# First batch's attention: transposes ahead of the fourth pair's scores, normalisation on GpSimd, copies shared with VectorE, one product matmul ahead of the last outputs

## The chip, the cores and the metric

The kernel runs on one core of a Trainium2 chip. Time is the device time of one launch in microseconds (us), the median of three runs. The engines are called as in the profile: PE is TensorE, DVE is VectorE, ACT is ScalarE, POOL is GpSimd, SP issues the DMAs. Each engine works through its own instructions in order and waits on semaphores for what the others produce.

## The reference

Two stages. The first is attention over 8 batches and 8 heads, sequence 576, head dimension 64, with a window of 32 keys: heads 0 to 3 look at the last 32 positions, heads 4 to 7 at every fourth of the last 128. The second is a dense feed-forward layer over all 4608 tokens, with an ELU between two products (512 to 2048 to 512), in float32.

```python
scores = scale * np.matmul(q, k.transpose(0, 1, 3, 2))
mask_plain = (rel >= 0) & (rel < window)
mask_dil = (rel >= 0) & (rel < window * dilation) & (rel % dilation == 0)
scores = np.where(masks[None, :, :, :], scores, -1000000000.0)
attn = np.exp(scores - np.max(scores, axis=-1, keepdims=True))
attn = attn / (np.sum(attn, axis=-1, keepdims=True) + 1e-09)
x = np.matmul(attn, v)                      # then to 4608 x 512
h = x @ w_in
g = np.where(h > 0.0, h, np.exp(np.minimum(h, 0.0)) - 1.0)
out = g @ w_out
```

## The kernel before, in words

**Feed-forward.** The tokens are worked in 9 chunks of 512 (`for c in range(NCH)`, L377), each in 16 blocks of the hidden dimension (L382). A block is a first product into the PSUM tile `h_ps` (`gemm1`, L271), ELU on ACT and DVE (`elu`, L282), and a second product into the four tiles `o_ps` (`gemm2`, L298), two blocks later. Chunk 0 multiplies float32 weights directly; from chunk 1 on, weights and activations are split into a high and a low part, and three products are added. The activations are split by `split_x` (L257): ACT casts to `xh` (L267), DVE takes the difference `xl` (L268). For chunk 1 it is called when the loop comes to that chunk, but its pieces of early columns are free to go as soon as their input is there.

**Weights.** They arrive as 64-bit floats and are put together as float32: the magnitude on ACT (`magnitude`, L98), then four DVE operations on bits (`convert`, L106 to L111). They are handled in pairs of two 128x512 blocks. In the order below pair 0 is converted in two halves (B0 for the first block of hidden units, C0 for the second) and pair 1 whole (D1); the others follow inside the loop.

**Attention of the first batch.** Eight heads are worked as four pairs. `first_attention` (L181) is a generator with five steps for a pair, and L348 gives the order in which the steps are issued, since everything in it is kept in program order on each engine: S (scores with the mask on PE, into PSUM tile `a` or `b`), M (row maximum and subtraction on DVE, L198 and L201; exp on ACT, L203), P (row sums, reciprocal and multiplication on DVE, L205, L169 to L171), T (12 transposing matmuls against the identity, L214, into `c` or `a`; then copies from PSUM into one of two tiles `pt`, eight per pair, on ACT, L223, or DVE, L221), O (12 output matmuls into `d` or `b`, L157; two copies into `x32` on ACT, L161 or L164). A is the magnitude of a weight pair on ACT, B, C and D its conversion on DVE. M of pairs 1 to 3 also starts the load of the weights (`load_w(hp, mx)`, L200), behind a small POOL copy (L84).

**Later batches.** Attention of batch c+1 is issued between the blocks of chunk c (L397). It has an order of its own, made by a scheduler, and its multiplication is on DVE for batch 1 and on POOL from batch 2 on (L243).

The identity is made on POOL at L339. PSUM tiles of the first batch come from the pool `ps_f`, which is closed before `ps_h`, `ps_o` and `ps_a` are opened (L357 to L360).

Of the kernel before, what the change touches and what calls it, by code (L numbers as in the profile page):

```python
# [10 lines left out]
F32 = mybir.dt.float32  # L11
# [5 lines left out]
ALU = mybir.AluOpType  # L17
# [6 lines left out]
P = 128  # L24
G = 32
QB = 3 * G
NU = S // QB
NPAIR = H // 2
NA = 3
GU = QB // G  # L30
TC = 512
# [13 lines left out]
def body(ctx: ExitStack, tc: tile.TileContext, q, k, v, masks, w_in, w_out, out):  # L45
# [5 lines left out]
    fp = ctx.enter_context(tc.tile_pool(name="fp", bufs=3))  # L51
    ps_first = ExitStack()
    ps_f = ps_first.enter_context(tc.tile_pool(name="ps_f", bufs=1, space=bass.MemoryType.PSUM))


    masks_sb = const.tile([QB, 2 * NU * 2 * G + QB], BF16, name="masks_sb")
# [20 lines left out]
    def mm(*args, **kw):  # L77
        inorder(nc.tensor.matmul(*args, **kw))  # L78
# [102 lines left out]
    def first_attention(hp, loaded):  # L181

        dil = hp >= NPAIR // 2
        qt, kt, vt = loaded
        if hp >= 2:
            sm = early[2 * (hp - 2) + 1][:QB, 2 * NU * D:2 * NU * (D + 2 * G)].rearrange("p (u j) -> p u j", u=2 * NU)
        else:
            sm = ap.tile([QB, 2 * NU, 2 * G], F32, name="sm")
        mx = ap.tile([QB, 2 * NU], F32, name="nmx", bufs=4)
        sums = ap.tile([QB, 2 * NU], F32, name="sums", bufs=4)  # L190
        s_ps = ps_f.tile([P, 2, TC], F32, name="ab"[hp % 2])[:QB, :, :NU * 2 * G]
        for h in range(2):
            mm(s_ps[:, h, :], ones_sb, mask_sb[:, int(dil), :], start=True, stop=False)
        scores([s_ps[:, h, :] for h in range(2)], qt, kt, False)
        yield
        s4 = s_ps.rearrange("p h (n j) -> p h n j", n=NU)
        mx4 = mx.rearrange("p (h n) -> p h n", h=2)
        inorder(nc.vector.tensor_reduce(out=mx4, in_=s4, op=ALU.max, axis=mybir.AxisListType.X))  # L198
        if hp > 0:
            load_w(hp, mx)  # L200
        inorder(nc.vector.tensor_tensor(out=sm.rearrange("p (h n) j -> p h n j", h=2), in0=s4,  # L201
                                        in1=mx4.unsqueeze(3).broadcast_to([QB, 2, NU, 2 * G]), op=ALU.subtract))
        inorder(nc.scalar.activation(out=sm, in_=sm, func=AF.Exp, scale=0.125))  # L203
        yield
        inorder(nc.vector.tensor_reduce(out=sums, in_=sm, op=ALU.add, axis=mybir.AxisListType.X))  # L205
        last_step[hp] = normalise(nc.vector, sm, sums, inorder).ins
        yield
        tr = transposed()

        t_ps = ps_f.tile([P, 2, TC], F32, name="ca"[hp % 2])  # L210
        for n in range(NU):
            for h in range(2):
                o = n % NA * QB
                mm(t_ps[h * 2 * G:(h + 1) * 2 * G, n // NA, o:o + QB], sm[:, h * NU + n, :], ident, start=True, stop=True)  # L214
        t4 = t_ps[:, :, :NA * QB].rearrange("p i (n q) -> p i n q", n=NA)
        for h in range(2):
            to = tr[:, h * NU:(h + 1) * NU, :].rearrange("p (i n) q -> p i n q", i=2)
            for c, r, m in ((0, 0, 2), (1, 0, 1), (1, 1, 1), (2, 0, 2)):
                cs, ks, rs = slice(c * G, (c + 1) * G), slice((c + r) * G, (c + r + m) * G), slice((h * 2 + r) * G, (h * 2 + r + m) * G)
                if hp == NPAIR - 1 and h == 1:  # L220
                    inorder(nc.vector.tensor_copy(out=to[ks, :, :, cs], in_=t4[rs, :, :, cs]))  # L221
                else:
                    inorder(nc.scalar.copy(out=to[ks, :, :, cs], in_=t4[rs, :, :, cs]))  # L223
        yield
        a_ps = ps_f.tile([P, 2, TC], F32, name="db"[hp % 2])
        yield outputs(0, hp, [(a_ps[:, i, :], i * NA, (i + 1) * NA) for i in range(NU // NA)], vt, tr, inorder)
# [41 lines left out]
                nc.vector.tensor_tensor(out=xl[hp][:, u], in0=src, in1=xh[hp][:, u].bitcast(F32), op=ALU.subtract)  # L268
                t0 += n

    def gemm1(c, f):  # L271
        h_ps = ps_h.tile([P, TC], F32, name="h_ps")
        i = 2 * f
        if c == 0:
            terms = [(full[i], x32[0][:, n, :TC], n) for n in range(NC)]
        else:
            terms = [(wh[i], x[n], n) for n in range(NC) for x in (xh, xl)] + [(wl[i], xh[n], n) for n in range(NC)]
        for t, (w, x, n) in enumerate(terms):
            mm(h_ps, w[:, n * P:(n + 1) * P], x, start=t == 0, stop=t == len(terms) - 1)
        return h_ps  # L280

    def elu(h_ps, first):  # L282
# [52 lines left out]
    for what in "m0 qk0 qk1 qk2 qk3 v0 v1 w0 v2 v3".split():  # L335
        i = int(what[-1])
        if what[0] == "m":
            nc.sync.dma_start(out=masks_sb, in_=masks)
            nc.gpsimd.tensor_copy(out=ident, in_=ones_sb)  # L339
        if what[0] == "w":  # L340
            load_w(i)
        for t, src in zip("qkv", (q, k, v)):
            if t in what:
                nc.sync.dma_start(out=rooms[i]["qkv".index(t)], in_=src[i])
    x32[0] = xp.tile([P, NPAIR, S], F32, name="x32", bufs=2)
    its = [first_attention(hp, rooms[hp]) for hp in range(NPAIR)]

    for what in "S0 S1 M0 M1 A0 S2 S3 P0 M2 T0 P1 M3 T1 O0 P2 T2 O1 P3 B0 T3 O2 O3 A1 C0 D1".split():  # L348
        i = int(what[1])
        if what[0] == "A":  # L350
            inorder(magnitude(i))
        elif what[0] in "BCD":
            last_conversion = convert(i, inorder, {"B": slice(0, DM), "C": slice(DM, 2 * DM), "D": slice(0, 2 * DM)}[what[0]])
        else:
            last_copy = next(its[i])
    ready = 2
    ps_first.close()  # L357
    ps_h = ctx.enter_context(tc.tile_pool(name="ps_h", bufs=2, space=bass.MemoryType.PSUM))
    ps_o = ctx.enter_context(tc.tile_pool(name="ps_o", bufs=TC // P, space=bass.MemoryType.PSUM))
    ps_a = ctx.enter_context(tc.tile_pool(name="ps_a", bufs=1, space=bass.MemoryType.PSUM))  # L360
    loaded[1, 0] = load_pair(1, 0)
# [13 lines left out]
                store(c, o_of.pop(c))  # L375

    for c in range(NCH):  # L377
        if c > 0:
            split_x(c)
        att = batch_attention(c + 1) if c + 1 < B else iter(())  # L380
        emitted = 0
        for f in range(NF):  # L382
            while c == 0 and ready < min(NF, f + AHEAD):
                with tc.issue_after(below[-1] if below else last_copy.ins):
                    magnitude(ready)
                with tc.issue_after(last_conversion.ins):
                    last_conversion = convert(ready)
                if ready + NR < NF:
                    load_w(ready + NR)
                ready += 1  # L390
            while c == 1 and split < min(NF, f + 2):

                with tc.issue_after(hidden[-4 if split < 2 else -1]):
                    split_w(split)
                split += 1
            pend.append((c, f, elu(gemm1(c, f), c == 0)))
            while emitted < (f + 1) * STEPS // (NF - 1):  # L397
                emitted += 1
                if c == 0 and emitted <= 2:
                    with tc.issue_after(last_step[NPAIR - 1]):  # L400
                        next(att, None)
                else:
                    next(att, None)
            flush(LAG)
# [60 lines left out]
```

## Time and profile before

| | |
|---|---|
| median of 3 runs | 923.32 us (921.7 to 923.71) |
| profiled execution | 923.31 us, span 921.5 us |
| PE busy | 902.1 us, 98% of the span |
| DVE, ACT, POOL busy | 525.9, 391.9, 42.2 us |
| first product matmul of chunk 0 starts | 34.08 us |

The span is the time from the first to the last recorded instruction; 1.8 us of the profiled execution lie around it. Times in the trace count from the span's start. PE is close to full, so the reading goes to the stretch before the first product, in which it is not. A matmul in float32 leaves two records in the trace: 12 matmuls are 24 records, a product of four matmuls is 8.

### The profile page before, as it was taken

The numbers are of one execution on the slowest core, as the hardware profiler recorded it, in microseconds if no ns is written. First come the engines' busy times: TensorE is split into PE (matmuls) and PEld (weight loads), VectorE is DVE, ScalarE is ACT, GpSimd is POOL, SyncE is SP. The second block draws the span as 40 slices with busy tenths as digits, with TensorE's granted clock in tenths as the row PEclk, the third lists the DMA queues.
The fourth block names the chain that finished last, engine by engine and source line by source line (L and its number), as shares of the span: only waits on it lengthen the run. The fifth ranks groups of instructions, "written<-read, shape, count | busy, mean of one in ns | idle before, by whom it ended". The sixth has DMA issues, their size and how long they took to land.

```text
span 921.5 us, 15903 instructions
## 1 busy us (share of the span) xinstructions
PE 902.1 (98%) x6504; PEld 688.3 (75%) x6504; DVE 525.9 (57%) x912; ACT 391.9 (43%) x1185; POOL 42.2 (5%) x34
## 2 busy tenths in 40 slices
PE   6799999999999999999999999999999999999998
PEld 4444445788878887888878887888788888888886
DVE  6699885965565545655475546655655443343332
ACT  4756762543344345344444335443443432233222
POOL 1000000010000000000010001000000000000000
PEclk8899999999999999999999999999999999999999
DMA  9964010211121112111211102111300010001001
GB/s 349 380 232 136 17 44 18 100 44 45 35 100 44 38 42 73 44 45 46 78 55 45 43 21 98 44 45 35 100 18 18 1 47 0 1 1 46 1 0 46
DMA packets 23800, 59.38 MB, mean 64 GB/s; under 512 B 2640, under 2 KB 2736, under 8 KB 23728
## 3 DMA queue, kind: packets, MB, share of 16 engines
q1 hardware_dynamic: 23728, 58.37, 18.7%
q8 instruction: 51, 0.84, 0.4%
q14 instruction: 21, 0.17, 0.1%
HBM read 48.92 MB, written 9.44 MB: 63 GB/s over the span
## 4 chain that ended last, share of the span: by engine, by line
PE 90%; ACT 5%; DVE 3%; DMA 1%; issue 1%; SPq 0%; ACTq 0%; DVEq 0%
PE h_ps L78 42%; PE o_ps L78 41%; PE a_ps L78 6%; ACT sm L242 3%; ACT pt L223 1%; DMA kt<-k 1%; PE b L78 1%; DVE sm L238 1%; DVE nmx L239 1%; ACT e L284 0%; DVE e L291 0%; ACT r L119 0%; ACT o L309 0%; DVE e L290 0%; PE c L78 0%
## 5 line engine op out<-in xcount | busy, mean ns | idle before, releaser
L78 PE MATMUL o_ps<-a,gh 128*128 128x512 f32 x640 | 258.4, 432 | 0.0
L78 PE MATMUL o_ps<-r,gh 128*128 128x512 f32 x512 | 205.8, 402 | 0.4
L78 PE MATMUL h_ps<-xh,r 128*128 128x512 f32 x512 | 200.5, 392 | 0.0
L78 PE MATMUL o_ps<-r,gl 128*128 128x512 f32 x512 | 199.7, 390 | 0.0
L78 PE MATMUL h_ps<-xl,r 128*128 128x512 f32 x512 | 199.3, 389 | 0.0
L284 ACT ACTIVATE e<-h_ps 128x512 f32<-128x512 f32 x144 | 85.5, 594 | 241.9 <-PE h_ps L78 241.7
L294 ACT CAST gh<-e 128x512 fp32r<-128x512 f32 x128 | 79.5, 621 | 191.2 <-DVE e L291 191.2
L290 DVE TENSOR_SCALAR e<-e 128x512 f32<-128x512 f32 x128 | 61.5, 481 | 164.1 <-ACT e L284 163.3
L78 PEld LDWEIGHTS o_ps<-a,gh 128*128 128x128 f32 x640 | 119.8, 188 | 45.8 <-issue 26.3
L295 DVE TENSOR_TENSOR gl<-e,gh 128x512 fp32r<-128x512 f32 x128 | 88.5, 692 | 75.0 <-PE o_ps L78 58.0
L242 ACT ACTIVATE sm<-sm,nmx 96x64 f32<-96x64 f32 x336 | 112.0, 335 | 32.0 <-DVE nmx L240 31.5
L78 PE MATMUL h_ps<-xh,a 128*128 128x512 f32 x448 | 119.7, 389 | 0.0
L78 PEld LDWEIGHTS o_ps<-r,gh 128*128 128x128 f32 x512 | 96.0, 187 | 26.2 <-ACT o L309 2.5
L78 PEld LDWEIGHTS o_ps<-r,gl 128*128 128x128 f32 x512 | 96.1, 188 | 21.1
L78 PEld LDWEIGHTS h_ps<-xh,r 128*128 128x128 f32 x512 | 96.1, 188 | 20.8 <-issue 0.2
L78 PEld LDWEIGHTS h_ps<-xl,r 128*128 128x128 f32 x512 | 96.1, 188 | 20.7 <-issue 0.7
L248 DVE STREAM_TRANSPOSE pt<-sm 32x384 f32<-32x384 f32 x168 | 95.5, 568 | 12.8 <-POOL sm L171 10.8
L78 PEld LDWEIGHTS h_ps<-xh,a 128*128 128x128 f32 x448 | 84.1, 188 | 17.5
L291 DVE SCALAR_TENSOR_TENSOR e<-h_ps,e 128x512 f32<-128x512 f32 x128 | 88.4, 691 | 3.9
L171 POOL TENSOR_TENSOR sm<-sm,sums 96x768 f32<-96x768 f32 x24 | 39.1, 1630 | 662.3 <-ACT e L284 321.6
L242 ACT ACTIVATION_READ_ACCUMULATOR sm<-sm,nmx 96x1 f32 x336 | 62.9, 187 | 0.0
L78 PE MATMUL h_ps<-x,a 128*128 128x512 f32 x128 | 60.3, 617 | 1.8 <-DVE gh L288 1.1
(82 smaller groups left out, 539.3 us busy)
## 6 DMA issues: line engine op xcount, KB each, us to landing
vt<-v SPq DMA_DIRECT2D x30, 384.0 KB, 3.2
kt<-k SPq DMA_DIRECT2D x30, 304.0 KB, 4.1
qt<-q SPq DMA_DIRECT2D x30, 288.0 KB, 3.6
r<-w_in SPq DMA_DIRECT2D x16, 512.0 KB, 7.0
r<-w_out SPq DMA_DIRECT2D x16, 512.0 KB, 7.1
out<-o SPq DMA_DIRECT2D x32, 256.0 KB, 2.9
out<-xl SPq DMA_DIRECT2D x4, 256.0 KB, 2.1
r<-v SPq DMA_DIRECT2D x2, 384.0 KB, 9.0
```

The lines of the kernel that those rows point to most:

```text
L78: inorder(nc.tensor.matmul(*args, **kw))
L171: return keep(eng.tensor_tensor(out=sm, in0=sm, in1=sums.unsqueeze(2).broadcast_to([QB, 2 * NU, 2 * G]), op=ALU.mult))
L223: inorder(nc.scalar.copy(out=to[ks, :, :, cs], in_=t4[rs, :, :, cs]))
L238: nc.vector.tensor_tensor(out=sm[:, h * NU:(h + 1) * NU, :].rearrange("p n j -> p (n j)"), in0=s_ps[h], in1=mask_sb[:, int(dil), :], op=AL ...
L239: nc.vector.tensor_reduce(out=nmx, in_=sm, op=ALU.max, axis=mybir.AxisListType.X)
L242: nc.scalar.activation(out=sm[:, u, :], in_=sm[:, u, :], func=AF.Exp, bias=nmx[:, u:u + 1], scale=0.125, accum_out=sums[:, u:u + 1])
L248: nc.vector.transpose(out=tr[ks, :, cs], in_=sm[cs, :, rs])
L284: nc.scalar.activation(out=e, in_=h_ps, func=AF.Exp)
L290: nc.vector.tensor_scalar(out=e, in0=e, scalar1=1.0, scalar2=-1.0, op0=ALU.min, op1=ALU.add)
L291: nc.vector.scalar_tensor_tensor(out=e, in0=h_ps, scalar=0.0, in1=e, op0=ALU.max, op1=ALU.add)
L294: nc.scalar.copy(out=gh, in_=e)
L295: nc.vector.tensor_tensor(out=gl, in0=e, in1=gh.bitcast(F32), op=ALU.subtract)
```

## The change

1. The order of the first batch's steps is another one. T0 stands before S3; P2 before M3; A0 behind M3 instead of behind M1; B0 behind T3 instead of before it.
2. The multiplication of pairs 0 to 2 goes to POOL; pair 3 keeps DVE.
3. The identity is made by a multiplication on POOL instead of a copy.
4. Of the copies behind the transposes, DVE takes over two of pair 1 (`c == 2`) and four of pair 2 (`h == 1`); it already had four of pair 3.
5. The transposes of pairs 0 and 2 get a PSUM pool of their own, `ps_c`. It is closed after B0, and `ps_h` is opened in its place, so that the first product's tile is there early.
6. The first product is a generator (`product1`), and one matmul of it (G0) is issued before the output step of pair 3 (O3).
7. `split_x(1)` is held behind the fourth last hidden block of chunk 0.

```diff
--- before.py
+++ after.py
@@ -51,6 +51,8 @@
     fp = ctx.enter_context(tc.tile_pool(name="fp", bufs=3))
     ps_first = ExitStack()
     ps_f = ps_first.enter_context(tc.tile_pool(name="ps_f", bufs=1, space=bass.MemoryType.PSUM))
+    ps_second = ExitStack()
+    ps_c = ps_second.enter_context(tc.tile_pool(name="ps_c", bufs=1, space=bass.MemoryType.PSUM, side="right"))
 
 
     masks_sb = const.tile([QB, 2 * NU * 2 * G + QB], BF16, name="masks_sb")
@@ -203,11 +205,13 @@
         inorder(nc.scalar.activation(out=sm, in_=sm, func=AF.Exp, scale=0.125))
         yield
         inorder(nc.vector.tensor_reduce(out=sums, in_=sm, op=ALU.add, axis=mybir.AxisListType.X))
-        last_step[hp] = normalise(nc.vector, sm, sums, inorder).ins
+        last = normalise(nc.vector if hp == NPAIR - 1 else nc.gpsimd, sm, sums, inorder)
+        if hp == NPAIR - 1:
+            last_step[hp] = last.ins
         yield
         tr = transposed()
 
-        t_ps = ps_f.tile([P, 2, TC], F32, name="ca"[hp % 2])
+        t_ps = (ps_c, ps_f)[hp % 2].tile([P, 2, TC], F32, name="ca"[hp % 2])
         for n in range(NU):
             for h in range(2):
                 o = n % NA * QB
@@ -217,7 +221,7 @@
             to = tr[:, h * NU:(h + 1) * NU, :].rearrange("p (i n) q -> p i n q", i=2)
             for c, r, m in ((0, 0, 2), (1, 0, 1), (1, 1, 1), (2, 0, 2)):
                 cs, ks, rs = slice(c * G, (c + 1) * G), slice((c + r) * G, (c + r + m) * G), slice((h * 2 + r) * G, (h * 2 + r + m) * G)
-                if hp == NPAIR - 1 and h == 1:
+                if hp >= 2 and h == 1 or hp == 1 and c == 2:
                     inorder(nc.vector.tensor_copy(out=to[ks, :, :, cs], in_=t4[rs, :, :, cs]))
                 else:
                     inorder(nc.scalar.copy(out=to[ks, :, :, cs], in_=t4[rs, :, :, cs]))
@@ -268,7 +272,8 @@
                 nc.vector.tensor_tensor(out=xl[hp][:, u], in0=src, in1=xh[hp][:, u].bitcast(F32), op=ALU.subtract)
                 t0 += n
 
-    def gemm1(c, f):
+    def product1(c, f):
+
         h_ps = ps_h.tile([P, TC], F32, name="h_ps")
         i = 2 * f
         if c == 0:
@@ -277,6 +282,11 @@
             terms = [(wh[i], x[n], n) for n in range(NC) for x in (xh, xl)] + [(wl[i], xh[n], n) for n in range(NC)]
         for t, (w, x, n) in enumerate(terms):
             mm(h_ps, w[:, n * P:(n + 1) * P], x, start=t == 0, stop=t == len(terms) - 1)
+            yield h_ps
+
+    def gemm1(c, f):
+        for h_ps in first if (c, f) == (0, 0) else product1(c, f):
+            pass
         return h_ps
 
     def elu(h_ps, first):
@@ -336,7 +346,7 @@
         i = int(what[-1])
         if what[0] == "m":
             nc.sync.dma_start(out=masks_sb, in_=masks)
-            nc.gpsimd.tensor_copy(out=ident, in_=ones_sb)
+            nc.gpsimd.tensor_tensor(out=ident, in0=ones_sb, in1=ones_sb, op=ALU.mult)
         if what[0] == "w":
             load_w(i)
         for t, src in zip("qkv", (q, k, v)):
@@ -345,17 +355,23 @@
     x32[0] = xp.tile([P, NPAIR, S], F32, name="x32", bufs=2)
     its = [first_attention(hp, rooms[hp]) for hp in range(NPAIR)]
 
-    for what in "S0 S1 M0 M1 A0 S2 S3 P0 M2 T0 P1 M3 T1 O0 P2 T2 O1 P3 B0 T3 O2 O3 A1 C0 D1".split():
+
+    for what in "S0 S1 M0 M1 S2 P0 M2 T0 S3 P1 P2 M3 A0 T1 O0 P3 T2 O1 T3 O2 B0 G0 O3 A1 C0 D1".split():
         i = int(what[1])
+        if what == "G0":
+            ps_second.close()
+            ps_h = ctx.enter_context(tc.tile_pool(name="ps_h", bufs=2, space=bass.MemoryType.PSUM, side="right"))
+            first = product1(0, 0)
         if what[0] == "A":
             inorder(magnitude(i))
         elif what[0] in "BCD":
             last_conversion = convert(i, inorder, {"B": slice(0, DM), "C": slice(DM, 2 * DM), "D": slice(0, 2 * DM)}[what[0]])
+        elif what[0] == "G":
+            next(first)
         else:
             last_copy = next(its[i])
     ready = 2
     ps_first.close()
-    ps_h = ctx.enter_context(tc.tile_pool(name="ps_h", bufs=2, space=bass.MemoryType.PSUM))
     ps_o = ctx.enter_context(tc.tile_pool(name="ps_o", bufs=TC // P, space=bass.MemoryType.PSUM))
     ps_a = ctx.enter_context(tc.tile_pool(name="ps_a", bufs=1, space=bass.MemoryType.PSUM))
     loaded[1, 0] = load_pair(1, 0)
@@ -375,7 +391,10 @@
                 store(c, o_of.pop(c))
 
     for c in range(NCH):
-        if c > 0:
+        if c == 1:
+            with tc.issue_after(hidden[-4]), tc.issue_after(below[-4]):
+                split_x(c)
+        elif c > 1:
             split_x(c)
         att = batch_attention(c + 1) if c + 1 < B else iter(())
         emitted = 0
```

The instruction orders show where this lands. The first place is the PE around the first transposes; `c<-ident,sm` are the transposes of pair 0, `b<-r_79` (before) and `b<-r_82` (now) the scores of pair 3. Before:

```order
L78 MATMUL a<-r_77 32x64 x36
L78 LDWEIGHTS masks_sb
L78 MATMUL b<-masks_sb 96x384
L78 LDWEIGHTS masks_sb
L78 MATMUL b<-masks_sb 96x384
L78 MATMUL b<-r_79 32x64 x36
L78 MATMUL c<-ident,sm 64x96 x12
```

Now:

```order
L80 MATMUL a<-r_80 32x64 x36
L80 MATMUL c<-ident,sm 64x96 x12
L80 LDWEIGHTS masks_sb
L80 MATMUL b<-masks_sb 96x384
L80 LDWEIGHTS masks_sb
L80 MATMUL b<-masks_sb 96x384
L80 MATMUL b<-r_82 32x64 x36
L80 MATMUL a<-ident,sm 64x96 x12
```

The transposes of pair 0 moved ahead of the mask matmuls and scores of pair 3, which now stand behind them.

The second place is DVE around the normalisation of pair 3, whose sums are read from `r_80` (before) and `r_83` (now). Copies into `pt` are those behind transposes, a `TENSOR_SCALAR` of 128x512 is the beginning of a half conversion of weight pair 0. Before:

```order
L171 TENSOR_TENSOR r_78<-r_78,sums 96x768
L205 TENSOR_REDUCE sums<-r_80 96x12
L169 TENSOR_SCALAR sums<-sums 96x12
L170 RECIPROCAL sums<-sums 96x12
L171 TENSOR_TENSOR r_80<-r_80,sums 96x768
L106 TENSOR_SCALAR a_201<-a_201 128x512
L108 TENSOR_SCALAR a_201<-a_201 128x512
L109 SCALAR_TENSOR_TENSOR a_201<-r_101,a_201 128x512
L268 TENSOR_TENSOR xl_1183<-x_106,xh_1182 128x64
L111 SCALAR_TENSOR_TENSOR a_201<-r_101,a_201 128x512
L268 TENSOR_TENSOR xl_1189<-x_106,xh_1188 128x64
L221 COPY pt_75<-a 64x6x32
```

Now:

```order
L225 COPY pt_78<-a 64x6x32 x2
L207 TENSOR_REDUCE sums<-r_83 96x12
L171 TENSOR_SCALAR sums<-sums 96x12
L172 RECIPROCAL sums<-sums 96x12
L173 TENSOR_TENSOR r_83<-r_83,sums 96x768
L225 COPY pt_79<-c 64x6x32
L225 COPY pt_79<-c 32x6x32 x2
L225 COPY pt_79<-c 64x6x32
L225 COPY pt_78<-a 64x6x32
L225 COPY pt_78<-a 32x6x32 x2
L225 COPY pt_78<-a 64x6x32
L108 TENSOR_SCALAR a_333<-a_333 128x512
```

Two copies of pair 1 (`pt_78<-a`, first row) stand ahead of pair 3's sums, four of pair 2 and four of pair 3 behind its multiplication, and the conversion begins behind all of them. The differences `xl` are gone from here.

The third place is the PE around the first product; `a<-ident` are the transposes of pair 3, `d` and `b` the outputs of pairs 2 and 3, `h_ps` the product. Before:

```order
L78 MATMUL b<-pt_75,vt 64x96 x12
L78 MATMUL a<-ident,r_80 64x96 x12
L78 MATMUL d<-pt_76,r_78 64x96 x12
L78 MATMUL b<-pt_75,r_80 64x96 x12
L78 MATMUL h_ps<-x_106,a_201 128x512 x8
L78 MATMUL a_ps_558<-kt,qt 32x64
```

Now:

```order
L80 MATMUL a<-ident,r_83 64x96 x12
L80 MATMUL d<-pt_79,r_81 64x96 x12
L80 MATMUL h_ps<-x_109,a_333 128x512
L80 MATMUL b<-pt_78,r_83 64x96 x12
L80 MATMUL h_ps<-x_109,a_333 128x512 x7
L80 MATMUL a_ps_562<-kt,qt 32x64
```

One of the eight matmuls of the first two products moved ahead of the twelve output matmuls of pair 3.

## Rows read from the trace of the kernel before

**Rows 1.** the page, busy time of each engine.

```profile
PE 902.1 (98%) x6504; PEld 688.3 (75%) x6504; DVE 525.9 (57%) x912; ACT 391.9 (43%) x1185; POOL 42.2 (5%) x34
```

**Rows 2.** four windows; columns: stretch, us, busy us of each engine, granted clock, DMA share, GB/s.

```profile
29.20:32.50 3.30, 1.14 (x21) 0.93 (x22) 2.19 (x7) 1.86 (x6) 0.00 (x0) 1.00 1.03 408
34.08:39.30 5.22, 5.22 (x6) 2.19 (x7) 4.15 (x7) 3.18 (x4) 0.00 (x0) 0.50 1.01 401
44.00:99.00 55.00, 55.00 (x354) 25.55 (x337) 53.12 (x76) 33.51 (x97) 0.00 (x0) 1.00 0.47 159
99.00:150.00 51.00, 49.95 (x250) 23.16 (x249) 36.09 (x52) 31.22 (x70) 0.00 (x0) 1.00 0.12 36
```

**Rows 3.** chain of waits, in order of time; columns: start us, us, what.

```profile
18.39 0.31 ACT pt L223
...
25.22 0.24 ACT xh L267
...
34.08 9.71 PE h_ps L78 x16
```

**Rows 4.** timeline of PE; columns: start us, us, work [idle before and releaser].

```profile
13.85 0.87 PE L78 MATMUL b<-masks_sb 96*96 96x384 bf16 x2 [3.62 <-DVE sm L171]
...
16.11 2.19 PE L78 MATMUL c<-ident,sm 96*64 96x96 f32 x24
...
25.49 1.23 PE L78 MATMUL a<-ident,r 96*64 96x96 f32 x23
```

**Rows 5.** timeline of DVE in the attention of the first batch.

```profile
12.26 0.95 DVE L171 TENSOR_TENSOR sm<-sm,sums 96x768 f32<-96x768 f32 x1
...
18.28 0.95 DVE L201 TENSOR_TENSOR r<-b,nmx 96x768 f32<-96x768 f32 x1
...
21.89 0.95 DVE L205 TENSOR_REDUCE sums<-r 96x12 f32<-96x768 f32 x1 [0.34 <-ACT r L203]
...
24.21 0.42 DVE L106 TENSOR_SCALAR a<-a 128x512 f32<-128x512 f32 x1
...
25.86 0.69 DVE L111 SCALAR_TENSOR_TENSOR a<-r,a 128x512 uint32<-128x512 uint32 x1
...
30.23 1.48 DVE L221 COPY pt<-a 64x192 f32<-64x192 f32 x4 [1.00 <-ACT pt L223]
...
35.09 0.69 DVE L106 TENSOR_SCALAR a<-a 128x1024 f32<-128x1024 f32 x1 [1.00 <-ACT a L98]
...
41.69 0.69 DVE L288 SCALAR_TENSOR_TENSOR gh<-h_ps,e 128x512 f32<-128x512 f32 x1 [1.99 <-ACT e L286]
```

**Rows 6.** timeline of ACT in the same stretch.

```profile
16.27 1.15 ACT L98 ACTIVATE a<-r 128x1024 f32<-128x1024 f32 x1 [4.49 <-DMA r<-w_in]
...
21.88 2.59 ACT L223 COPY pt<-a 64x192 f32<-64x192 f32 x8
...
33.92 3.21 ACT L98 ACTIVATE a<-r 128x1024 f32<-128x1024 f32 x3
```

**Rows 7.** POOL's first multiplication from its timeline, then all of them on the page.

```profile
172.53 1.93 POOL L171 TENSOR_TENSOR sm<-sm,sums 96x768 f32<-96x768 f32 x1 [154.03 <-ACT gh L294]
...
L171 POOL TENSOR_TENSOR sm<-sm,sums 96x768 f32<-96x768 f32 x24 | 39.1, 1630 | 662.3 <-ACT e L284 321.6
```

**Rows 8.** a DVE tensor-scalar beside POOL's, then all of them on the page.

```profile
173.38 1.36 DVE L290 TENSOR_SCALAR e<-e 128x512 f32<-128x512 f32 x1 [0.26 <-ACT e L284]
...
L290 DVE TENSOR_SCALAR e<-e 128x512 f32<-128x512 f32 x128 | 61.5, 481 | 164.1 <-ACT e L284 163.3
```

**Rows 9.** later product blocks on PE, and one DVE row.

```profile
44.63 3.70 PE L78 MATMUL h_ps<-x,a 128*128 128x512 f32 x8
...
51.60 3.60 PE L78 MATMUL h_ps<-x,a 128*128 128x512 f32 x8
...
105.75 3.70 PE L78 MATMUL h_ps<-x,a 128*128 128x512 f32 x8 [1.05 <-DVE gh L288]
...
100.05 0.17 DVE L169 TENSOR_SCALAR sums<-sums 96x12 f32<-96x12 f32 x1 [2.24 <-ACT sm L242]
```

## The prediction

> **What bounds the kernel now.** I read the page's busy shares first: PE is busy 902.1 us of 921.5 [rows 1]. So the time is the start of the big products plus the PE's own work, and any edit ahead of them counts only by when the products run. [...] The chain of waits says what sets 34.08: from 18.39 it runs through ACT's copies of the transposed attention weights, eight of about 0.32 us per pair, with output copies and casts of 0.24 between them, then DVE's copies of the last pair, that pair's outputs and their copies, and at 34.08 the first products, 16 records of 9.71 us [rows 3]. The timelines of PE, DVE and ACT then give me a start time for each step that the change moves [rows 4 to 6]. From 44 to 99 DVE is busy 53.12 of 55.00 [rows 2], so a late DVE there can hold the PE later on.
>
> **What the change removes from that chain.** Two copies of the second pair's and four of the third's go from ACT to DVE, and the casts of 0.24 go later: 6 x 0.32 + 3 x 0.24 = 2.6 us off ACT between 18 and 31 us. DVE loses three multiplications of 0.95 [rows 5]. That is what speaks for a gain. What follows is where this time is lost again, step by step, in the order of the changed program.
>
> *First transposes ahead of the fourth pair's scores.* They need pair 0's multiplication. DVE's part of that step ends where the multiplication started before, at 12.26 [rows 5]; POOL's takes 1.93 the first time in the trace and 1.63 in the mean of its 24 [rows 7], so about 14.1. No row shows one beside this stage's DVE work; from below I bound it by DVE's 0.95 and from above by 3.9, twice the longest row, and take 1.9, since the rows are of the same shape. What DVE may lose beside POOL has a row too: a tensor-scalar of 128x512 took 1.36 where its mean is 0.48, and ended 0.3 after POOL's multiplication beside it [rows 7, 8]. Here only 12-element tensor-scalars of that kind lie beside POOL, and the 0.9 that one might lose falls into an idle stretch of DVE (below); I cost it at nothing. The PE issued its next instruction at 13.85 although what it waits for had long been there (idle 3.62 behind a multiplication that had ended at 13.21), so little is to be had below 13.85. Then 2.19 of transposes and 2.3 of scores, as from 13.85 to 16.11 before [rows 4]: the scores end at about 18.5 where they ended at about 16.2. DVE's reduce and subtraction behind them (twice 0.95) end at 20.4, where they ended at 19.23 [rows 5]. The fourth exp on ACT then ends at 21.3; before, the copies behind it began at 21.88 [rows 6].
>
> [...]
>
> *The magnitude of the first weights (1.15 us).* Before it filled a gap in which ACT had been idle 4.49 us [rows 6]. Now it stands between the fourth exp and the second pair's copies: they start at 22.4 instead of 21.88.
>
> *Two of the second pair's copies on DVE.* They stand ahead of the fourth pair's sums in DVE's order, and each waits for the ACT copies written before it. With ACT's six at 0.32 from 22.4 and DVE's two after its third and sixth, DVE is free at about 24.9. Before, the fourth pair's normalisation ran from 21.89 until the conversion behind it at 24.21 [rows 5], released by its exp. Now it runs 24.9 to 27.2: 3 us later. This is the step that I trust most, since DVE idles from 20.4 to about 23 for it.
>
> *Last pair's transposes.* They ran at 25.49 [rows 4], now from 27.2. They take 1.23, or 2.2 at the lower clock [rows 4]; ACT's four copies 1.3, half of the eight in 2.59 [rows 6]; DVE's four 1.48 behind them [rows 5]. DVE ends at 31.2 to 32.2, before 31.71. All that ACT saved is spent here.
>
> *First half of the first weights' conversion.* Before it ran at 24.21 to 26.55, in front of those copies [rows 5]. Now it is behind them, 2.3 us more: 33.5 to 34.5. The first product matmul waits for it, and the last pair's outputs stand behind that matmul on the PE.
>
> *The first product block ahead of the outputs.* From 34.08 to 39.31 the PE worked at half clock, which is 2.6 us of full-clock work on products. I take the same clock up to 39.3, because the PE idles no less before it (2 to 3 us here, 2.16 of 3.30 there). In the changed kernel one product matmul (0.90 at full clock, 8 records in 3.60 [rows 9], twice that at half) and the outputs (24 records as the transposes, 2.2 at half) end at 37.5 to 38.5, and until 39.31 the next gives 0.4 to 0.9: 1.3 to 1.8 us of product work in place of 2.6. So the products come out of this **0.8 to 1.3 us late; I take 1.1**.
>
> *DVE behind it.* The second weights' magnitudes on ACT stand behind the last output copies: before at 33.92 [rows 6], now at about 38.2 to 39.2 (0.7 of copies); DVE's conversion of them runs from about 40.4 at the latest instead of 35.09, 5.3 us later. Before, DVE idled 1.99 us soon after [rows 5], and the products that need it are themselves 1.1 later, so at most 5.3 - 2.0 - 1.1 = 2.2 us of DVE lateness is left for a stretch with 1.9 us to spare (55.00 less 53.12), plus the 2.24 of idle at 97.8 to 100.0. The one place where DVE makes the PE wait is 1.05 us at 105.75 [rows 9]. Bounds 0 to 2.2; I take 1.0, the nearer to that row, because the next chunk's casts and differences have also left this stretch. They come back around 125 to 135 us, where DVE is busy 36.09 of 51.00 us [rows 2], so I cost them at nothing; without that cover it would be some 0.5.
>
> Sum: 1.1 + 1.0 = 2.1 us on the profiled 923.31 (921.5 of span and 1.8 around it), which equals the median of 923.32 to 0.01. **Forecast 925.4 us**, its own range 924.1 to 926.8.
>
> **Rivals.**
> *The clock stays full.* For it: the PE starts its products earlier relative to the outputs and the change puts work into its gap. With the first product at 32.2 to 33.5 (DVE's second-pair copies not holding the fourth pair, or holding it less) at full clock, 0.9 of product and 1.3 of outputs leave 3.6 to 4.9 us for the rest until 39.31; in all 4.5 to 5.8 against 2.6. That is 1.9 to 3.2 faster: 920.1 to 921.4, say 920.8. Against it: 3.30 us with 1.14 of work was followed by half clock in the trace of before [rows 2], and the gap is not smaller now.
>
> *Nothing to be told apart.* DVE's copies find ACT's already done, the fourth pair is ready by 24.5, the first product starts at 32.2 at half clock, the outputs end at 36.1, and 2.5 us of product work are done by 39.31: the same as before. DVE's lateness (about 0.9) goes into its idle 1.99. 923.3 to 924.2, say 923.7. For it: ACT has 2.6 us less to do. Against it: the order of waits in DVE's queue.
>
> *POOL late with the first pair (slower).* The first transposes wait for POOL and the fourth scores stand behind them, so each us beyond 14.1 at which pair 0 is ready goes one for one into scores, fourth exp and the whole chain. At twice the longest row (3.9) this is 2.0 more: 927.5. Against it: the rows are of the same shape and differ by 0.3 only [rows 7].
>
> **How the numbers follow.** About 0.2% (1.85 us) is what a measurement of this kernel tells from no change: below 921.5 is faster, above 925.2 slower. The forecast has 0.50, of which 0.36 lie above 925.2 and 0.14 below. The clock rival has 0.20 (0.18 faster, 0.02 same), the rival with no difference 0.20 (0.17 same, 0.03 slower), the late POOL 0.10 (all slower). Faster 0.18, same 0.33, slower 0.49. The range 920.6 to 928.0 takes in the clock rival but its fastest part and the POOL rival at its row-based price.
>
> **What would show it.** In the changed kernel's DVE timeline: an idle stretch of 2 us or more before the second pair's two copies, and the fourth pair's sums after 24 us. Conversion of the first weights' first half ending after 33.3, and the first product matmul right behind it. In the windows view: clock 0.50 up to about 39.3. The third product starting 1 to 1.5 us later than 44.63 [rows 9], and a wait of the PE for DVE's hidden values that is longer than 1.05 near 105. Wrong I would be if the fourth pair's sums start before 22.5, if the clock is full from 34 on, or if POOL's first multiplication ends after 15.

## The result

The changed kernel takes 926.53 us (926.12 to 927.23, 5 runs) where the kernel before took 923.44 (5 runs): ratio 1.0034, 95% interval 1.0022 to 1.0046, so 3.1 us slower. The forecast was 925.4 in a range of 920.6 to 928.0. The profiled execution's span is 924.4 us, 2.9 more than before.

### The profile after

The PE's timeline of the changed kernel, with the columns of [rows 4]:

```profile
14.62 1.91 PE L80 MATMUL c<-ident,sm 96*64 96x96 f32 x24 [2.85 <-POOL sm L173]
...
17.27 1.39 PE L80 MATMUL b<-r 64*32 64x64 f32 x72
...
28.04 2.19 PE L80 MATMUL a<-ident,r 96*64 96x96 f32 x24 [0.34 <-DVE r L173]
29.99 2.16 PE L80 MATMUL d<-pt,r 128*64 128x96 f32 x24
35.61 2.05 PE L80 MATMUL h_ps<-x,a 128*128 128x512 f32 x2 [3.46 <-DVE a L113]
37.59 1.81 PE L80 MATMUL b<-pt,r 128*64 128x96 f32 x24
39.32 6.28 PE L80 MATMUL h_ps<-x,a 128*128 128x512 f32 x14
...
46.59 3.70 PE L80 MATMUL h_ps<-x,a 128*128 128x512 f32 x8
...
108.74 3.70 PE L80 MATMUL h_ps<-x,a 128*128 128x512 f32 x8 [2.08 <-DVE gh L298]
```

The first transposes start at 14.62 and the fourth pair's scores now end at 18.66. The last transposes start at 28.04 (25.49 in [rows 4]). Between pair 2's outputs, which end at 32.15, and the first product matmul at 35.61 the PE idles 3.46 us, released by the last operation of the half conversion. The outputs of the last pair come behind that matmul, and the other 14 product records start at 39.32, where all 16 had started at 34.08 [rows 3]. The third product starts at 46.59 instead of 44.63, and a later product waits 2.08 us for DVE's hidden values where it waited 1.05 [rows 9].

DVE's timeline shows where the time before 35.61 goes:

```profile
16.92 0.80 DVE L171 TENSOR_SCALAR sums<-sums 96x12 f32<-96x12 f32 x1
...
19.74 0.95 DVE L203 TENSOR_TENSOR r<-b,nmx 96x768 f32<-96x768 f32 x1
23.73 0.35 DVE L225 COPY pt<-a 64x192 f32<-64x192 f32 x1 [3.03 <-ACT pt L227]
25.11 0.36 DVE L225 COPY pt<-a 64x192 f32<-64x192 f32 x1 [1.03 <-ACT pt L227]
25.50 0.95 DVE L207 TENSOR_REDUCE sums<-r 96x12 f32<-96x768 f32 x1
...
31.63 1.48 DVE L225 COPY pt<-a 64x192 f32<-64x192 f32 x4 [2.35 <-ACT pt L227]
33.12 0.43 DVE L108 TENSOR_SCALAR a<-a 128x512 f32<-128x512 f32 x1
...
34.77 0.69 DVE L113 SCALAR_TENSOR_TENSOR a<-r,a 128x512 uint32<-128x512 uint32 x1
...
41.20 0.69 DVE L108 TENSOR_SCALAR a<-a 128x1024 f32<-128x1024 f32 x1 [3.49 <-ACT a L100]
```

Two idle stretches matter. DVE is done with the fourth pair's subtraction at 20.69 and idles 3.03 us before the second pair's first copy, then 1.03 before the second, each time until ACT's copies are there. ACT's fourth copy in turn waits 0.48 us for DVE's first. Only then come the fourth pair's sums, at 25.50 instead of 21.89 [rows 5]. The last copies run at 31.63, and the half conversion, which ran at 24.21 in [rows 5], runs from 33.12 to 35.46. The second conversion starts at 41.20 instead of 35.09.

The windows view, with the columns of [rows 2], has the granted clock:

```profile
34.08:39.30 5.22, 3.69 (x26) 2.12 (x26) 3.50 (x6) 0.00 (x0) 0.00 (x0) 0.67 0.62 241
...
35.60:39.30 3.70, 3.69 (x26) 2.10 (x26) 2.01 (x4) 0.00 (x0) 0.00 (x0) 0.56 0.45 169
```

From 35.6 to 39.3 the PE is busy all the time at a mean of 0.56, and at 0.50 until 38.80, where before it had 0.50 up to 39.30 [rows 2]. The clock was low already ahead of the idle 3.46 us, at 0.51 from 28.00 to 32.15, and at 0.98 in the idle stretch itself. POOL's timeline:

```profile
3.11 0.34 POOL L349 TENSOR_TENSOR ident<-masks_sb 96x96 f32<-96x96 bf16 x1 [0.32 <-DMA masks_sb<-masks]
...
13.10 1.47 POOL L173 TENSOR_TENSOR sm<-sm,sums 96x768 f32<-96x768 f32 x1 [2.21 <-DVE sums L172]
...
16.22 1.47 POOL L173 TENSOR_TENSOR sm<-sm,sums 96x768 f32<-96x768 f32 x1 [1.52 <-DVE sums L172]
```

The identity takes 0.34 us and the first large multiplication 1.47, where the first of before took 1.93 [rows 7]; that multiplication starts 0.15 us behind the end of DVE's reciprocal (12.72 plus 0.23), so there is no late start on POOL. DVE's 12-element tensor-scalar at 16.92 took 0.80, where the one at 15.64 took 0.17, and ended at 17.72, 0.03 us after POOL's multiplication beside it. The 1.36 us one of [rows 8] had ended 0.28 us after POOL's [rows 7]. The longer time costs nothing here, as DVE then idles 0.78 us for the fourth pair's scores.

### The profile page after: what moved, and what is told of

It is laid out like the page before. It is cut to its first block, busy times and chain, and to the rows that moved or that the text cites. A ratio compares the mean times of both kernels' runs of the same rounds, so it can differ in the third digit from the quotient of the medians.

```text
span 924.4 us, 15911 instructions
## 1 busy us (share of the span) xinstructions
PE 903.0 (98%) x6504; PEld 689.9 (75%) x6504; DVE 525.3 (57%) x915; ACT 389.7 (42%) x1179; POOL 46.6 (5%) x37
## 3 DMA queue, kind: packets, MB, share of 16 engines
HBM read 48.92 MB, written 9.44 MB: 63 GB/s over the span
## 4 chain that ended last, share of the span: by engine, by line
PE 84%; DVE 9%; ACT 4%; issue 2%; DMA 1%; SPq 0%; POOL 0%; ACTq 0%; DVEq 0%; POOLq 0%
PE o_ps L80 39%; PE h_ps L80 39%; PE a_ps L80 5%; ACT sm L246 3%; DVE a L111 1%; DVE a L113 1%; DVE pt L252 1%; DVE nmx L243 1%; DVE sm L242 1%; DVE a L108 1%; DVE a L110 1%; PE b L80 1%; DMA kt<-k 1%; DVE e L301 0%; ACT e L294 0%
## 5 line engine op out<-in xcount | busy, mean ns | idle before, releaser
L173 POOL TENSOR_TENSOR sm<-sm,sums 96x768 f32<-96x768 f32 x26 | 42.0, 1617 | 667.7 <-ACT e L294 321.6
```

The lines of the kernel that those rows point to most:

```text
L173: return keep(eng.tensor_tensor(out=sm, in0=sm, in1=sums.unsqueeze(2).broadcast_to([QB, 2 * NU, 2 * G]), op=ALU.mult))
```

## Experiments

Theory: DVE's order makes the loss. The second pair's copies hold the fourth pair, the half conversion stands behind the last copies, and the single product matmul and the outputs behind it wait for that. Rivals: the product matmul ahead of the outputs is a loss in itself; the first transposes ahead of the fourth scores are; the move to POOL or the later split is. Each kernel was timed 5 to 11 times, next to the kernel before on the same chip, whose median was 923.62, 924.06 and 924.39 in the three sets (runs 1 to 4, 5 to 8, 9 to 12), so ratios are compared.

Three numbers of each trace are listed beside the time: the start of DVE's reduce for the second pair's maximum (8.96 in the kernel before), the start of the third product (44.63 in [rows 9]) and the longest wait of a product for DVE's hidden values (1.05). The last column has the sum of the latter two less that of before, then the span less that of before.

| run | median us | ratio (95%) | second pair's reduce | third product | wait | sum, span: less before |
|---|---|---|---|---|---|---|
| the change | 926.53 | 1.0034 (1.0022 to 1.0046) | 9.69 | 46.59 | 2.1 | +3.0, +2.9 |
| 1 second pair's copies on ACT | 925.16 | 1.0012 (1.0004 to 1.0021) | 9.71 | 44.43 | 1.9 | +0.7, +0.8 |
| 2 conversion early | 919.66 | 0.9954 (0.9941 to 0.9966) | 9.47 | 41.38 | 0.4 | -3.9, -3.6 |
| 3 product matmul behind | 923.81 | 0.9999 (0.9990 to 1.0008) | 9.59 | 44.26 | 1.6 | +0.2, +0.5 |
| 4 sums first and conversion early | 919.13 | 0.9945 (0.9932 to 0.9959) | 9.54 | 41.36 | 0.4 | -3.9, -4.1 |
| 5 as 2, product matmul behind | 922.33 | 0.9981 (0.9972 to 0.9990) | 10.07 | 42.66 | 1.7 | -1.3, -1.0 |
| 6 as 4, normalising on DVE | 921.63 | 0.9968 (0.9957 to 0.9979) | 10.38 | 43.66 | 0.4 | -1.6, -1.2 |
| 7 as 4, fourth scores first | 919.61 | 0.9946 (0.9934 to 0.9959) | 9.44 | 41.48 | 0.4 | -3.8, -3.6 |
| 8 as 4, split as before | 921.04 | 0.9962 (0.9949 to 0.9976) | 10.11 | 41.74 | 0.9 | -3.0, -2.7 |
| 9 the change, idle filled | 924.05 | 0.9998 (0.9989 to 1.0007) | 9.57 | 45.76 | 0.4 | +0.5, +0.8 |
| 10 before, idle filled | 921.66 | 0.9972 (0.9961 to 0.9982) | 9.16 | 41.67 | 1.7 | -2.3, -1.9 |
| 11 before, product matmul ahead | 919.44 | 0.9946 (0.9934 to 0.9959) | 9.73 | 40.39 | 0.9 | -4.4, -3.9 |
| 12 best version | 917.09 | 0.9921 (0.9908 to 0.9935) | 9.41 | 38.37 | 1.2 | -6.1, -6.1 |

The third product and the wait account for every span to 0.5 us. So the change acts by when the products run, and by one wait for DVE in chunk 0, and by nothing later of more than 0.5 us. The second pair's reduce comes ahead of every step that was moved and follows the landing of the inputs; it differs by up to 1.4 us between the traces. A smaller difference between two third products can come from there, so the parts are judged by the ratios of the medians.

### 1 to 4: which order on DVE

Run 1 takes the second pair's copies back to ACT:

```diff
-                if hp >= 2 and h == 1 or hp == 1 and c == 2:
+                if hp >= 2 and h == 1:
```

> The changed kernel, but the second pair's two copies are back on ACT. Theory (DVE's order): the fourth pair's sums start right behind its exp, near 21.7 instead of 25.50; the last transposes then wait only for the PE's outputs of pair 1 (about 26.7 instead of 28.04), DVE's last copies end near 30.7, the half conversion near 33.0, and the first product matmul starts at 33.0 instead of 35.61. At half clock half of that is worth something by 39.3: 924.0 to 925.3 us. Rival (the product matmul ahead of the outputs is the loss): the outputs stay behind it, 926.0 to 926.8. Rival (first transposes ahead of the fourth scores): no change, 926.5.

Its DVE and its PE:

```profile
22.03 0.95 DVE L207 TENSOR_REDUCE sums<-r 96x12 f32<-96x768 f32 x1 [0.91 <-ACT r L205]
...
31.09 0.43 DVE L108 TENSOR_SCALAR a<-a 128x512 f32<-128x512 f32 x1
...
33.58 1.41 PE L80 MATMUL h_ps<-x,a 128*128 128x512 f32 x2 [3.10 <-DVE a L113]
```

The sums came at 22.03, 3.5 us sooner, but the conversion only 2.0 sooner, since it still waits for the last copies, which wait for ACT. The time is 0.2% less than that of the change: the hold is real, and undoing it gives back less than run 2's edit does.

Run 2 puts only the half conversion back in front of the last transposes and copies:

```diff
-... T1 O0 P3 T2 O1 T3 O2 B0 G0 O3 ...
+... T1 O0 P3 T2 O1 B0 T3 O2 G0 O3 ...
```

> The changed kernel, but the first half conversion stands ahead of the last pair's transposes and copies again (as before). Theory (DVE's order): conversion at 29.3 to 31.6 instead of 33.12 to 35.46, the first product matmul follows pair 2's outputs at about 32.2 without the idle 3.46 us, the outputs of the last pair end near 35.8 instead of 39.4, and 3.5 us at half clock to full clock are gained: 923.0 to 924.8 us. Rival (the product matmul ahead of the outputs): a smaller gain, 925.5 or more, since the outputs still stand behind it. Rival (first transposes first): 926.5.

The PE's timeline of run 2, and its window:

```profile
29.79 2.06 PE L80 MATMUL d<-pt,r 128*64 128x96 f32 x24
31.78 1.13 PE L80 MATMUL h_ps<-x,a 128*128 128x512 f32 x2
32.84 1.33 PE L80 MATMUL b<-pt,r 128*64 128x96 f32 x24
34.10 6.28 PE L80 MATMUL h_ps<-x,a 128*128 128x512 f32 x14
...
34.08:39.30 5.22, 5.22 (x14) 2.39 (x13) 4.30 (x6) 5.06 (x8) 0.00 (x0) 1.00 0.97 359
```

The product matmul follows pair 2's outputs without a gap, the outputs follow it, the rest starts at 34.10, and the clock is full from there on (1.00 up to 39.30). The second pair's copies still hold the fourth pair, whose sums start at 25.30. That is 5.2 us at the third product and 1.7 in the later wait, more than expected, because the clock was expected to stay low until 39.3. This one move turns 0.3% slower into 0.5% faster.

Run 3 moves the product matmul behind the outputs and leaves the late conversion:

```diff
-... T3 O2 B0 G0 O3 A1 ...
+... T3 O2 B0 O3 G0 A1 ...
```

> The changed kernel, but the single product matmul stands behind the last pair's outputs again. Theory (DVE's order): the outputs run at 33.2 to 35.0, the products start at 35.5 when the conversion ends, so about 1.9 us of product work instead of 0.9 by 39.3, and the magnitudes on ACT and the second conversion on DVE start some 3.5 us sooner, which takes the added wait near 108 away: 924.3 to 925.3 us, still slower than before. Rival (the product matmul ahead of the outputs is the loss): all of it comes back, 923.3.

The PE's timeline of run 3:

```profile
33.43 2.18 PE L80 MATMUL b<-pt,r 128*64 128x96 f32 x22 [0.73 <-DVE pt L225]
35.80 7.62 PE L80 MATMUL h_ps<-x,a 128*128 128x512 f32 x16 [0.19 <-DVE a L113]
```

The outputs no longer wait for the conversion, and the products start together at 35.80. The loss is gone (0.9999): 923.81 us lies between the theory's 924.3 and the rival's 923.3. Taken alone that speaks for the rival; run 5 decides.

Run 4 mends both orders and keeps every other edit:

```diff
-... M3 A0 T1 O0 P3 T2 O1 T3 O2 B0 G0 O3 ...
+... M3 A0 P3 T1 O0 T2 O1 B0 T3 O2 G0 O3 ...
```

> The changed kernel with both of DVE's orders mended and every other edit kept: the fourth pair's normalisation ahead of the second pair's transposes and copies, the first half conversion ahead of the last transposes. Theory (DVE's order): sums near 21.7, the first product matmul at 30.5 to 32, outputs done near 33 to 34; the PE has no idle stretch of 3 us left. At half clock up to 39.3 this is 2.5 us less than now, 923.0 to 924.5; if the clock stays full, 5 to 6 us less, 920 to 921.5. Rival (the product matmul ahead of the outputs): 925.5 or more. Rival (first transposes first): 926.5.

DVE's timeline of run 4:

```profile
21.85 0.95 DVE L207 TENSOR_REDUCE sums<-r 96x12 f32<-96x768 f32 x1 [0.91 <-ACT r L205]
...
24.28 0.35 DVE L225 COPY pt<-a 64x192 f32<-64x192 f32 x1
25.66 0.36 DVE L225 COPY pt<-a 64x192 f32<-64x192 f32 x1 [1.03 <-ACT pt L227]
...
29.15 0.43 DVE L108 TENSOR_SCALAR a<-a 128x512 f32<-128x512 f32 x1
```

The sums run at 21.85, the copies behind them, but the conversion only at 29.15, since third-pair copies stand before it. It is 0.9945, within the interval of run 2 and faster than was expected even at full clock: with the conversion early, the place of the sums no longer shows.

### 5: is the product matmul ahead of the outputs a loss?

Run 2 with the matmul behind the outputs (`... B0 T3 O2 O3 G0 ...`).

> As the run with the early conversion (919.66 us), but with the single product matmul behind the last pair's outputs. There the matmul ran 31.78 to 32.91, while DVE made the last copies that the outputs wait for (they end at 32.91). Theory now (the conversion's place decides, and the matmul in the gap keeps the PE's clock full): without it the PE idles about 1.1 us, outputs at 33.0, products at 34.4; 920.5 to 921 if the clock stays full, 922 to 923.5 if it falls. Rival (the product matmul ahead of the outputs is a loss in itself, 926.53 to 923.81 when it was moved behind): 917 to 919.

The PE of run 5, its wait for hidden values, and its window:

```profile
33.56 1.20 PE L80 MATMUL b<-pt,r 128*64 128x96 f32 x22 [0.81 <-DVE pt L225]
34.70 7.13 PE L80 MATMUL h_ps<-x,a 128*128 128x512 f32 x16
...
PE h_ps L80 <- DVE gh L298: 1.7, 1, 1.7
...
34.08:39.30 5.22, 5.22 (x27) 2.70 (x24) 4.35 (x6) 4.46 (x7) 0.00 (x0) 1.00 0.98 359
```

Here the same matmul ahead of the outputs is worth 0.27% (0.9981 against 0.9954), where with a late conversion it cost 0.35%. The rival falls: the matmul is good where it fits into a wait, bad where it makes the outputs wait for its own input. The clock is full in both from 34.08 on (1.00 up to 39.30), so the gain is not the clock's: up to 1.28 us at the third product (run 5's trace started 0.60 later), and 1.3 in the wait near 105, which the expectation had left out. By that the time came out at 922.33 us, where 920.5 to 921 had been expected at full clock.

### 6 to 8: the other parts, undone one at a time in run 4

Run 6 has all multiplications on DVE, run 7 the fourth scores ahead of the first transposes, run 8 the split as before:

```diff
-        last = normalise(nc.vector if hp == NPAIR - 1 else nc.gpsimd, sm, sums, inorder)
+        last = normalise(nc.vector, sm, sums, inorder)
```
```diff
-... M1 S2 P0 M2 T0 S3 P1 ...
+... M1 S2 S3 P0 M2 T0 P1 ...
```
```diff
-        if c == 1:
-            with tc.issue_after(hidden[-4]), tc.issue_after(below[-4]):
-                split_x(c)
-        elif c > 1:
+        if c > 0:
```

> As the run with both orders mended (919.13 us), but all multiplications on DVE. Theory: the move to POOL is worth little: DVE has three times 0.95 more ahead of the fourth pair's subtraction, of which it idled 1.18 before that, so the fourth exp and all behind it come 1 to 1.7 us later; 919.5 to 920.8. Rival (POOL's late multiplication holds the first transposes, and their going first is a loss): 918 to 919.

> As the run with both orders mended (919.13 us), but with the fourth pair's scores ahead of the first pair's transposes again. Theory: neutral, since scores end 2 us earlier but ACT's copies of pair 0 end 1.7 later, and the fourth exp stands behind them at 21 to 22 either way: 918.8 to 920. Rival (first transposes first cost time): 917 to 918.5.

> As the run with both orders mended (919.13 us), but the split of the second chunk's activations is free to go early again. Theory: three casts of 0.24 come back into ACT's queue before the products and four differences of 0.22 into DVE's: 0.3 to 1 us later, 919.3 to 920.2. Rival (holding the split back costs time at the beginning of chunk 1): 918 to 919.

On DVE the normalisation makes it 0.23% slower (0.9968 against 0.9945), with the fourth pair's subtraction at 22.02 instead of 19.99. Of these 2.03 us 0.84 lie in the later start of that trace, so it is not shown that POOL is worth more than the 0.4 to 1.7 us that were expected. The order of scores and transposes is neutral (0.9946), as expected. The earlier split comes out 0.17% slower (0.9962), but the two intervals overlap by 0.0010, and its trace started 0.57 later, so only the longer wait for DVE, by 0.5 us, speaks for a cost. So none of these parts, undone beside the mended orders, is the loss: POOL is a gain, the later split perhaps one. The identity's multiplication was never undone alone; runs 2, 4 and 12 keep it and are faster than the kernel before.

### 9 and 10: does idle time cost again by the clock?

Run 9 leaves every wait of the changed kernel and puts 15 spare matmuls into the PE's idle stretch (`... O2 F8 F7 B0 G0 O3 ...`, where the number behind F is `i`); run 10 puts 10 into that of the kernel before (`... O2 F5 F5 O3 ...`, with the tile from `ps_f`). The code of run 9, cut to its loop:

```diff
+            filler = ps_c.tile([P, 2, TC], F32, name="c")
+            for _ in range(i):
+                mm(filler[:QB, 0, :NU * 2 * G], ones_sb, mask_sb[:, 0, :], start=True, stop=True)
```

> The changed kernel with 15 spare mask matmuls (0.23 us each at full clock, results unused) on the PE between pair 2's outputs and the single product matmul, where it idled 3.46 us. No wait is moved. Theory (idle time costs a second time by the granted clock behind it): the clock stays full behind 35.6, product matmul and outputs take 0.9 and 1.3 instead of 2.05 and 1.81, the rest starts near 37.8 instead of 39.32, and the second weights are converted 1.5 us sooner: 924 to 925.2 us. Rival (only the late conversion counts, the clock does not): 926.5 or more.

> The kernel before with 10 spare mask matmuls (results unused) on the PE between pair 2's and pair 3's outputs, where it idled 2.16 us. No wait is moved. Theory: products start at 34.1 as before but at full clock, 2.6 us of product work are won by 39.3, part of it lost to DVE, which is nearly full up to 99 us: 0.9970 to 0.9985 of the time before. Rival (the clock is not what idle time costs): 1.000.

Run 9 on the PE, and its clock:

```profile
32.36 3.86 PE L80 MATMUL c<-masks_sb 96*96 96x384 bf16 x15
36.28 1.13 PE L80 MATMUL h_ps<-x,a 128*128 128x512 f32 x2
37.34 1.21 PE L80 MATMUL b<-pt,r 128*64 128x96 f32 x24
38.48 6.28 PE L80 MATMUL h_ps<-x,a 128*128 128x512 f32 x14
...
36.20:39.30 3.10, 3.04 (x29) 1.81 (x29) 1.72 (x3) 0.71 (x3) 0.00 (x0) 1.00 0.30 123
```

The fillers even delay the product matmul (36.28 against 35.61), yet it takes 1.13 instead of 2.05, the outputs 1.21 instead of 1.81, and the kernel is 0.36% faster than the change (2.1 us by the two spans). The fillers did not keep a full clock here, since it was at 0.50 from 29.20 to 32.50, ahead of them; it is full behind them (1.00 from 36.20 to 39.30). Run 10:

```profile
29.10 2.04 PE L78 MATMUL c<-masks_sb 96*96 96x384 bf16 x10
...
33.71 7.13 PE L78 MATMUL h_ps<-x,a 128*128 128x512 f32 x16 [0.79 <-ACT x L161]
...
34.08:39.30 5.22, 5.22 (x13) 2.28 (x12) 4.50 (x6) 4.67 (x7) 0.00 (x0) 1.00 1.02 405
```

Products that start at 33.71 take 7.13 us for 16 records at full clock (1.00), where they took 9.71 [rows 3], and the kernel before gains 0.28% by work whose results nobody reads. 0.7 us of it goes back into the wait for DVE.

### 11 and 12: the useful part alone, and the best version

Run 11 is the kernel before with only the single product matmul ahead of the last outputs (`... B0 T3 O2 G0 O3 A1 ...`).

> The kernel before with one part of the change alone: the single product matmul ahead of pair 3's outputs (with the PSUM pools that this needs); the order of all other steps, the multiplications on DVE, the copies on ACT and the split are as before. There the conversion ended at 26.55, so the matmul goes into the gap at 29.3. Theory (the matmul is good where its conversion is early): the gap is filled by 0.9 us, the outputs start at 31.76 as before, the rest of the products follow with three of four matmuls left, and the clock may stay full: 0.9965 to 0.9990. Rival (the matmul ahead of the outputs is a loss in itself): 1.001 or more.

The PE's timeline of run 11:

```profile
29.38 1.12 PE L80 MATMUL h_ps<-x,a 128*128 128x512 f32 x2
30.44 0.38 PE L80 MATMUL b<-pt,r 128*64 128x96 f32 x2
31.98 1.20 PE L80 MATMUL b<-pt,r 128*64 128x96 f32 x22 [1.17 <-DVE pt L225]
33.12 6.28 PE L80 MATMUL h_ps<-x,a 128*128 128x512 f32 x14
```

The matmul goes into the gap before the outputs at 29.38, because the conversion is done by then, and the products go on at 33.12 at full clock (1.00 from 32.50 to 39.30). That is 0.9946, better than the 0.9965 to 0.9990 expected and as good as run 4, from one part of the change. Much of it is the clock: run 10's fillers brought the third product forward by 2.96 us in the same gap, the matmul by 4.24, so some 1.3 are an estimate of what the matmul gives by itself.

Run 12 has DVE do the sums and the half conversion before any copy that waits for ACT, and ACT the first magnitude before its first copies:

```diff
-... M2 T0 S3 P1 P2 M3 A0 T1 O0 P3 T2 O1 T3 O2 B0 G0 O3 ...
+... M2 A0 T0 S3 P1 P2 M3 P3 T1 O0 B0 T2 O1 T3 O2 G0 O3 ...
-                if hp >= 2 and h == 1 or hp == 1 and c == 2:
+                if hp >= 2 and h == 1:
```

> A version from what the runs showed: the changed kernel with the first magnitude ahead of the first copies, the fourth pair's normalisation ahead of the second pair's transposes, the second pair's copies all on ACT, and the half conversion ahead of the third pair's copies. DVE has then no wait for ACT before the conversion, which ends near 26.5, and the single product matmul follows pair 2's outputs at once, near 30. Theory: 0.5 to 1 us below the run with both orders mended, 0.993 to 0.9945. Rival (the last copies behind the transposes bound the outputs either way): 0.9945 to 0.996.

Its DVE, then its PE:

```profile
23.89 0.42 DVE L108 TENSOR_SCALAR a<-a 128x512 f32<-128x512 f32 x1
...
26.23 1.47 DVE L225 COPY pt<-c 64x192 f32<-64x192 f32 x4
...
28.89 1.12 PE L80 MATMUL h_ps<-x,a 128*128 128x512 f32 x2
29.95 1.21 PE L80 MATMUL b<-pt,r 128*64 128x96 f32 x24
31.09 6.28 PE L80 MATMUL h_ps<-x,a 128*128 128x512 f32 x14
```

The conversion ends at 26.21, the matmul, the outputs and the products follow each other without a gap, and the third product starts 6.3 us sooner than before. 917.09 us, ratio 0.9921, a little below the 0.993 to 0.9945 expected: it beats both kernels.

## Why the prediction was right

The direction, the place and the mechanism held: slower, by DVE's order ahead of the first product. By its steps:

- *First transposes on POOL's multiplication*: pair 0 ready at 14.57 (14.1 forecast), scores done at 18.66 (18.5), the subtraction at 20.69 (20.4). POOL took 1.47, not 1.9; DVE's part began later instead, as the second pair's reduce started at 9.69 where it had started at 8.96. That start follows the landing of the second pair's inputs (the PE waits 0.35 us for them at 8.09, where before its scores began at 7.49) and stands ahead of every moved step. It lay at 8.96 to 9.73 in the traces with the order of before and at 9.41 to 10.38 in those with a changed one; whether the change has a part in that is not shown.
- *Second pair's copies*: DVE free at 25.47 (24.9), the fourth pair done at 27.89 (27.2). Right in mechanism and nearly in size; that ACT's copies also wait for DVE's (0.48) was not in the forecast. But "the step that I trust most" is not what the loss hangs on: undone alone it gives back 0.2% (run 1), and with the conversion early undoing it no longer shows (run 4 against run 2).
- *Last copies and half conversion*: copies end at 33.11 (31.2 to 32.2), the conversion at 35.46 (33.5 to 34.5). The bound was too low by 0.9 us. Its terms were the transposes' 2.19 at a clock of 0.50 (from 16.10 to 18.30 before) and copies that follow at once; the transposes started 0.8 later than forecast. That this step is the decisive one (run 2) was not seen: it was counted with its 2.3 us, and with it early the clock is full from 34.08 on as well (1.00).
- *Product block ahead of outputs*: the rest of the products started at 39.32, the third product 1.96 us later than before. Forecast 0.8 to 1.3. This is the term that was too small, since the outputs ended at 39.40 and not at 37.5 to 38.5; up to 0.73 of that can be the later start of this trace. So the third product also lies beyond the 1 to 1.5 us that the prediction had named as its sign. The half clock up to about 39.3 came nearly as it was taken (0.50 from 35.60 to 38.80).
- *DVE behind it*: the wait near 105 went from 1.05 to 2.08, by 1.03. Forecast 1.0, from bounds of 0 to 2.2; that it fits so closely is luck.
- *Sum*: 1.96 + 1.03 = 3.0 against the 2.1 forecast; the spans differ by 2.9.

Of the rivals, the full clock did not come (0.56), but runs 2 and 4 show its case: the first product at 31.64 to 31.78, the clock at 1.00 from 32.50 to 39.30, and 919.1 to 919.7 us; its 920.1 to 921.4 was worked out for a start at 32.2 to 33.5. The rival without a difference fell with DVE's idle 3.03 us, the late POOL with 1.47.

What stays open: in runs 1 to 12 the clock between 12 and 32 us differs from kernel to kernel (from 29.20 to 32.50 it lies between 0.50 and 1.00) and is not explained here by rows. In the changed kernel it is at 0.52 from 25.00 to 29.20, where it was 1.00 before, so what first lowered it there is not known. Only the idle stretches between 28 and 36 us were tested by filling them.

## What to carry to other kernels

An engine that is kept in program order and takes over work from another also takes over that engine's waits, as DVE did with 3.03 and 1.03 us for ACT's copies: put ahead of such an operation whatever is ready and awaited elsewhere (here the fourth pair's sums and the half conversion), and only then the copies that wait. A matmul moved ahead into a gap is a gain if its operands are there before the gap begins, and a loss if the work behind it now waits for them; the same edit was worth 0.35% one way and 0.27% the other. Where the profile shows half clock behind an idle stretch, look for a cost beyond the idle time: with most of 2.16 us of idle filled by work of no use, the third product started 2.96 us sooner (run 10).

## What the runs showed of the hardware that was not expected

With spare matmuls in idle stretches of 2.16 and 3.46 us the granted clock is 1.00 behind them (without, 0.50 in the kernel before [rows 2] and 0.56 in the changed one). By the ratios they are worth 2.6 us in the kernel before and 3.3 in the changed one (1.9 and 2.1 by the spans), though they compute nothing that is used. A second point: a 12-element DVE tensor-scalar beside POOL's multiplication took 0.80 us in the changed kernel and ended 0.03 us after it. The same step of the third pair took 0.17 where DVE has the multiplication, in the kernel before at 20.13 and in run 11 at 20.91. DVE's subtraction at 13.80, beside POOL's first multiplication, kept its 0.95. Why the one took longer and the other did not, no run here shows.
